# A Hedgehog linear-attention and MLP stack on one core: the query features scale only one of their two softmax halves, and every queue gets a new order

## The chip, the core and the metric

The kernel runs on one NeuronCore of a Trainium2 chip. Five engines work side by side, each through its own in-order queue: PE (TensorE, matrix products), DVE (VectorE), ACT (ScalarE), POOL (GpSimd) and SP (SyncE), which issues every DMA of this kernel. The metric is the device time of one launch in microseconds (us); lower is better. PEld in the rows is the loading of PE's weights, which overlaps its products.

## The reference

Four residual blocks on a (1, 2048, 512) input: attention, MLP, attention, MLP, with the same weights both times.

```python
def _A_ref(x, wqkv, w_phi, wo):
    H = 32; Dh = D // H          # D = 512, Dh = 16
    q, k, v = ...                # x @ wqkv, split by kind and head
    pq = jnp.einsum("bhsd,hdf->bhsf", q, w_phi)
    pk = jnp.einsum("bhsd,hdf->bhsf", k, w_phi)
    phi_q = jnp.concatenate([_softmax(pq, axis=-1), _softmax(-pq, axis=-1)], axis=-1)
    phi_k = jnp.concatenate([_softmax(pk, axis=-1), _softmax(-pk, axis=-1)], axis=-1)
    kv = jnp.einsum("bhsf,bhsd->bhfd", phi_k, v)
    z  = jnp.einsum("bhsf->bhf", phi_k)
    num = jnp.einsum("bhqf,bhfd->bhqd", phi_q, kv)
    den = jnp.einsum("bhqf,bhf->bhq", phi_q, z)[..., None] + 1e-6
    o = num / den
    return o.transpose(...).reshape(B, S, D) @ wo

def _B_ref(x, w1, w2):           # 512 -> 1792 -> 512
    return jnp.maximum(x @ w1, 0) @ w2

x = x + _A_ref(_layernorm(x), ...);  x = x + _B_ref(_layernorm(x), ...)
x = x + _A_ref(_layernorm(x), ...);  x = x + _B_ref(_layernorm(x), ...)
```

A head's output is a quotient: a factor on both softmaxes of a query's head scales num and den alike, and cancels but for the guard 1e-6.

## The kernel before

The 2048 rows are 16 chunks of 128 rows. A number is split into a high and a low float16 half, and a product is three matmuls of halves (PAIRS), so that PE works in float16. Names end in the layer l (0 or 1) and the chunk c or the tile t of two chunks.

- **First stage.** Weights come in and are split (fold, split); each chunk is normalised and turned, and gives keys (pk), values (pv) and queries (pq). The keys' features (feature_map with psum=True) and values are summed over all chunks into kv (gather). Of a value's product pv the high half is copied out by ACT (L791), PE then subtracts it with a matmul by "minus" (L795), and ACT copies the rest (L797).
- **Query features** (look, feature_map with psum=False; 32 of them). Queries wait in DRAM (q_dram) and come back as ql. DVE takes the maximum and minimum of each head's 16 numbers (L690, L691), shifts (L696); ACT takes the exponentials of the two halves (L708, two instructions); DVE sums each half and takes reciprocals (L714, L715); ACT multiplies the 64 reciprocals by PHI = 2^15 (L719); POOL multiplies all 1024 exponentials by them (L723); ACT rounds to the high half (L730), POOL takes the low half (L734), and SP turns the result by a DMA transpose (L578) into pT. PE multiplies it with kv (numerators, L1019, tile pn), and DVE adds the guard and divides (L1027 to L1030, tiles dn and o).
- **MLP.** For most tiles a seven-product scheme replaces eight block products (hidden_by_seven, L1433, bank ph; out_by_seven, L1608). Sums of weight blocks are built on POOL in the first tiles (sums_of_weight, L1289, and sums_of_second, L1326), stored in DRAM (s_dram, t_dram) and fetched per step by one 512 KB DMA (s, L1391) into one of three buffers; a load can go out once PE has read the sums three steps back. Sums of activations (n_t, n_u) are turned by DMA transposes into freed weight halves (wq_h, wq_l, wk_h, wk_l).
- **Order.** The order of each engine's queue is written out in the table ORDER, one digit a task: its place among the tasks still to come in the order in which the program made them. The class Plan merges the five queues, with its own estimate of each task (the numbers in add) and of each transfer (landing): a first time until a DMA lands, and a time by which it follows the one before. SP works strictly in order, so a DMA whose data isn't ready holds all behind it.
- **Buffers.** CAPS says how many tiles of a kind there are: two p16 (the features' halves, keys' and queries' alike), two e, three w2 (which hold s).

Of the kernel before, what the change touches and what calls it, by code (L numbers as in the profile page):

```python
# [18 lines left out]
P = 128  # L19
# [25 lines left out]
PHI = 2.0 ** 15  # L45
KV_S = 2.0 ** -26
# [35 lines left out]
        "22a002300024222817029200224007262110g2g2200201j02h3015022220b0228102a59010622002200211023100522220020102"
        "20021102000201023000342320022002000221022000010011010",
    ACT:
        "31201104220030005c5ba099fm088c306053cc10jj2902md2cj1003mZq320j141Zj0m2kZf0j1500k3k0j26gn2m5j1136312k3Mj4"
        "1222ll4010m10130h3021102301cc041gg310002801cc002060201bj2216312c1110k8jjd80g0f69da080d7c460307010aaa0301"
        "c0b0fa020c650400d40309gg18020b03600080740200100020850033494104501011403a3480262303201110141023500820a053"
        "032000020431012057115c53022201131020220251131303231010350243242021010142832204b4590302533333343350030004"
        "182b716191071018111222015261553544512362605599909808807cc0ccf00ef0ie00f0e2420a1d10b709250968073433a39383"
        "393570250a1912100510383067096106608533504321003044239a003305200550002041700122100605210643021004033020g0"  # L90
        "0e010524010504008d0770999051f05300322030014255016ecb101990u80607p067605v56060ep583m406I05G950D70Q677Zp6M"
        "6ZmL7777Zh805608043Zo44ZY032Zj04Zh4ZQ400011011040ZEf302ZQ52ZO4036311ZZjf33ZE110302224000ZZ31005042300030"
        "32200l605520052033135100f3ZG30141022010Ze22Zs0115044011102330006055246004030004140332501027011302B001044"
        "00014140220160j501360240306021g4021100222103020105042370501302070024400524401004003320030220030220030201"
        "03022103302040302200303321403020130220403305103000000",
# [48 lines left out]
class Plan:  # L144
# [32 lines left out]
    def landing(self, t):  # L177

        if t.turn:
            return 2.0 + t.kb / 220, t.kb / 230  # L180
# [1900 lines left out]
```

## Time and profile before

| | |
|---|---|
| median of 3 runs | 964.04 us (963.81 to 964.42) |
| the profiled execution's own time | 963.83 us |
| its span, first to last instruction | 962.1 us |
| between the two | 1.7 us |
| granted TensorE clock over the span | 1.000 of full speed (2.4 GHz) |
| PE, DVE, POOL, ACT busy | 98%, 72%, 67%, 60% of the span |
| DMA engines busy, moved | 74.3% in queue q1, 183.38 MB |

The profile has the engines' busy times, the waits (who waited for whom, the total, how often, the longest), the chain of waits that ended last (start, length, who), groups of instructions by line and shape, and timelines. An idle engine that nobody waits for costs nothing.

### The profile page before, as it was taken

What the parts mean: (1) busy time and instruction counts of PE and PEld (TensorE: products, weight loads), DVE (VectorE), ACT (ScalarE), POOL (GpSimd) and SP (SyncE); (2) the same over time, 40 slices, a digit from 0 to 9 for tenths busy, and PEclk for the clock granted to TensorE, in tenths of its full rate; (3) what the DMA queues carried; (4) which work ended last, traced back from release to release, by engine and by line L of the source; (5) the groups of instructions that cost most, each with busy time, mean ns of one, the idle gap of its engine ahead of it and who ended that gap; (6) DMA issues with size and microseconds to landing.
All of it is one profiled execution on the core that took longest, in us unless ns stands there. A gap on an engine that the chain in (4) does not pass through costs nothing.

```text
span 962.1 us, 23668 instructions
## 1 busy us (share of the span) xinstructions
PE 947.4 (98%) x9372; PEld 659.7 (69%) x9372; DVE 694.8 (72%) x1408; ACT 573.6 (60%) x1121; POOL 647.5 (67%) x634
## 2 busy tenths in 40 slices
PE   8999999999999999999999999999999999999997
PEld 5544555666665766566677775566666889888997
DVE  6899978856876877766566678987886575665455
ACT  7999978654554636454375555465555565555553
POOL 2699877778685857555376647267578888777644
PEclk9999999999999999999999999999999999999999
DMA  9387858499869697788649864599999786886541
GB/s 334 90 223 197 194 157 224 95 197 217 206 156 233 164 268 158 175 224 214 155 155 253 254 189 112 199 248 228 222 221 252 184 186 170 188 169 172 134 139 66
DMA packets 251807, 183.38 MB, mean 191 GB/s; under 512 B 180656, under 2 KB 188080, under 8 KB 251696
## 3 DMA queue, kind: packets, MB, share of 16 engines
q1 hardware_dynamic: 251696, 181.87, 74.3%
q8 instruction: 73, 1.20, 0.5%
q14 instruction: 38, 0.31, 0.1%
HBM read 108.30 MB, written 30.15 MB: 144 GB/s over the span
## 4 chain that ended last, share of the span: by engine, by line
PE 91%; DMA 2%; ACT 2%; POOL 2%; DVE 1%; issue 1%; SPq 0%; DVEq 0%; POOLq 0%; ACTq 0%
PE ph L1433 23%; PE py L1549 14%; PE py L1608 12%; PE pw L650 8%; PE pk L650 8%; PE pv L650 8%; PE pq L650 8%; PE ph L1513 3%; PE pn L1019 2%; PE kv L816 1%; DMA s<-s_dram 1%; DMA st_k<-in_A_wqkv_dram 1%; DMA wk_h<-n_u 1%; POOL sums L1289 0%; POOL p_q L734 0%
## 5 line engine op out<-in xcount | busy, mean ns | idle before, releaser
L1549 PE MATMUL py<-w,h 128*128 128x512 f16 x690 | 174.2, 379 | 0.0
L1433 PEld LDWEIGHTS <-s 128*128 128x128 f16 x2352 | 151.3, 98 | 28.3 <-DMA s<-s_dram 2.2
L1446 ACT ACTIVATE sn<-ph 128x128 f32<-128x128 f32 x294 | 80.6, 274 | 146.3 <-PE ph L1433 143.2
L650 PEld LDWEIGHTS <-xT 128*128 128x128 f16 x900 | 86.8, 98 | 99.1 <-DMA xT<-n_a 1.4
L1433 PEld LDWEIGHTS <-w 128*128 128x128 f16 x1764 | 111.0, 98 | 15.0 <-DMA wk_h<-n_u 1.4
L1433 PE MATMUL ph<-yT,s 128*128 128x128 f16 x1176 | 97.6, 219 | 1.1 <-DVE ph L1452 1.1
L1433 PE MATMUL ph<-yT,w 128*128 128x128 f16 x1176 | 97.6, 219 | 0.0
L1452 DVE TENSOR_TENSOR ph<-ph,sn 128x128 f32<-128x128 f32 x98 | 29.3, 299 | 92.3 <-PE ph L1433 48.5
L1549 PEld LDWEIGHTS <-h 128*128 128x128 f16 x690 | 61.4, 98 | 49.2
L734 POOL TENSOR_TENSOR p_q<-e_q,p_q 128x1024 f16<-128x1024 f32 x32 | 71.4, 2230 | 21.0 <-ACT p_q L730 21.0
L723 POOL TENSOR_TENSOR e_q<-e_q,fm_q 128x1024 f32<-128x1024 f32 x32 | 62.5, 1957 | 33.8 <-ACT fm_q L719 33.5
L734 POOL TENSOR_TENSOR p_k<-e_k,p_k 128x1024 f16<-128x1024 f32 x30 | 68.7, 2288 | 20.6 <-ACT p_k L730 20.5
L650 PE MATMUL pw<-wo_h,oT 128*128 128x512 f16 x256 | 81.4, 379 | 0.2 <-ACT qs L886 0.2
L650 PE MATMUL pk<-wk_h,xT 128*128 128x512 f16 x256 | 81.3, 379 | 0.0
L650 PE MATMUL pv<-wv_h,xT 128*128 128x512 f16 x256 | 81.2, 379 | 0.0
L723 POOL TENSOR_TENSOR e_k<-e_k,fm_k 128x1024 f32<-128x1024 f32 x30 | 59.5, 1983 | 28.7 <-ACT fm_k L719 27.7
L650 PEld LDWEIGHTS <-oT 128*128 128x128 f16 x384 | 37.0, 98 | 41.4 <-issue 1.0
L1457 DVE TENSOR_TENSOR ph<-ph,sn 128x256 f32<-128x256 f32 x98 | 41.9, 427 | 31.1 <-PE ph L1433 30.6
L1608 PEld LDWEIGHTS <-h 128*128 128x128 f16 x648 | 59.1, 98 | 6.4
L1229 POOL TENSOR_TENSOR w<-r 128x256 f32<-128x256 f32 x41 | 31.4, 766 | 40.0 <-ACT r L1225 40.0
L650 PE MATMUL pq<-wq_h,xq 128*128 128x512 f16 x168 | 56.6, 379 | 0.1
L1608 PE MATMUL py<-w,h 128*128 128x256 f16 x324 | 53.0, 273 | 0.0
(279 smaller groups left out, 2419.4 us busy)
## 6 DMA issues: line engine op xcount, KB each, us to landing
s<-s_dram SPq DMA_DIRECT2D x98, 512.0 KB, 4.4
q_dram<-qs SPq DMA_DIRECT2D x28, 256.0 KB, 3.8
ql<-q_dram SPq DMA_DIRECT2D x28, 256.0 KB, 3.7
u<-t_dram SPq DMA_DIRECT2D x13, 512.0 KB, 4.5
xt_dram<-xT SPq DMA_DIRECT2D x21, 256.0 KB, 4.2
xq<-xt_dram SPq DMA_DIRECT2D x21, 256.0 KB, 3.9
xe<-in_A_x_dram SPq DMA_DIRECT2D x16, 256.0 KB, 4.4
x<-in_A_x_dram SPq DMA_DIRECT2D x16, 256.0 KB, 4.2
```

The source lines that it names most:

```text
L650: nc.tensor.matmul(pm.ap, xT.ap[:, a, k, :], W.ap[b][:, k, :], start=(k == 0 and i == 0), stop=(k == KC - 1 and i == 2))
L723: (nc.vector if fast else nc.gpsimd).tensor_tensor(e3, e3, sm.unsqueeze(2).to_broadcast([P, 2 * n, DH]), op=ALU.mult)
L734: (nc.vector if fast else nc.gpsimd).tensor_sub(part16(1, cols), part16(1, cols, ef), part16(0, cols))
L1019: nc.tensor.matmul(at()[:, g, :], pT.ap[:, a, 4 * i + g, :], r[b].ap[:, 4 * i + g, :], start=(j == 0), stop=(j == 2))
L1229: nc.gpsimd.tensor_sub(rf.ap[:, :2, :], r.ap.rearrange("p (a b) -> p a b", a=4)[:, ::3, :], block(1).unsqueeze(1).to_broadcast([P, 2, P]))
L1433: nc.tensor.matmul(at(r), weight_of(i, b, kk, s, summed), rows_of(y, i, a, kk), start=(first and kk == 0 and n == 0), stop=(kk == 1 and n ...
L1446: nc.scalar.activation(saved(i), at(2), AF.Copy)
L1452: add(DVE, 0.27, lambda: nc.vector.tensor_tensor(at(3), at(1), saved(2), op=ALU.add), reads=[(ph, 1), (sn, 2)], writes=[(ph, 3)], boost=10 ...
L1457: add(DVE, 0.40, lambda: nc.vector.tensor_tensor(wide(ph), wide(ph), wide(sn), op=ALU.add), reads=[(sn, 0), (sn, 1)], writes=[(ph, 0), (ph ...
L1513: nc.tensor.matmul(at()[:, j, cs.start * P:cs.stop * P], W1.at(b, k, slice(f * P, (f + 1) * P)), yT.ap[:, cs, a, k, :], stop=(k == KC - 1 ...
L1549: nc.tensor.matmul(py.ap, h[a].ap.rearrange("p j t -> p (j t)")[:, cols], W2.at(b, fs[j], slice(0, D)), start=(begins and j == k == 0), st ...
L1608: nc.tensor.matmul(py.ap[:, 256 * r:256 * r + 256], left[a], right[b], start=(s == 0 and r == 0 and k == 0), stop=(last and k == 2), skip_ ...
```

## The change

For query features alone (not psum), the e tile is laid out by halves: all 32 first softmaxes (positive side), then all 32 second ones. With s1 and s2 the sums of the exponentials e1 and e2 of a head, it gives e1 * HALF and e2 * (s1 / s2 * HALF) in place of e1 * PHI / s1 and e2 * PHI / s2, with HALF = PHI / 16: both halves of a head times s1 / 16. The guard in the divide gets the same factor, from a small tile eps of 32 numbers a row. The constants of Plan.landing are new, and all five strings of ORDER. The keys' features keep their steps. Line numbers after L43 are higher in the new kernel.

```diff
+HALF = PHI / DH
 ORDER = {
     PE:
-        "000033222242210032000770204413339122603847310830209001180032710013140020331403160D516201xx12v04314031012"
+        "000052222522200001100770204413331802153847319030b20302901a02211013510600161013G0F051401411w203314q031036"
...
     def landing(self, t):
         if t.turn:
-            return 2.0 + t.kb / 220, t.kb / 230
+            return 1.6 + t.kb / 170, t.kb / 193
         if t.work > 1.5:
-            return 4.8, 2.4
-        return 1.6 + t.kb / 250, t.kb / 385
+            return 4.4, 2.5
+        return 1.8 + t.kb / 230, t.kb / 306
...
-            "statf": 2, "statb": 2, "fmf": 2, "fmb": 2, "dn": 2, "v": 2, "piece": 3,
+            "statf": 2, "statb": 2, "fmf": 2, "fmb": 2, "eps": 3, "dn": 2, "v": 2, "piece": 3,
...
         def part16(j, cols, x=None):
             if not psum:
-                return p16.ap[:, j, cols] if x is None else x
+                return (p16.ap[:, j, cols] if x is None else x).rearrange(
+                    "p (h s f) -> p h s f" if x is None else "p (s h f) -> p h s f", s=2, f=DH)
...
-                eh = e.ap[:, h:h + n]
+                eh = e.ap[:, h:h + n] if psum else e.ap.rearrange("p h s f -> p (h s f)").rearrange(
+                    "p (s h f) -> p h s f", s=2, f=DH)
...
+            def ratios(of=piece_of):
+                sm, e3 = of()[2], of()[5]
+                nc.vector.tensor_reduce(sm, e3, axis=AX.X, op=ALU.add)
+                nc.vector.reciprocal(sm[:, H:], sm[:, H:])
+                nc.vector.scalar_tensor_tensor(sm[:, H:], sm[:, :H], HALF, sm[:, H:], op0=ALU.mult, op1=ALU.mult)
+
+            def raised(of=piece_of):
+                e3 = of()[5]
+                nc.scalar.activation(e3[:, :H], e3[:, :H], AF.Copy, scale=HALF)
+
+            def guard(of=piece_of):
+                eps.ap = eps.make()
+                nc.scalar.activation(eps.ap, of()[2][:, :H], AF.Copy, scale=DEN_EPS)
...
             def product(of=piece_of):
                 _, _, sm, _, _, e3, _ = of()
+                if not psum:
+                    nc.gpsimd.tensor_tensor(e3[:, H:], e3[:, H:], sm[:, H:].unsqueeze(2).to_broadcast([P, H, DH]),
+                                            op=ALU.mult)
+                    return
...
+            if not psum:
+                add(DVE, 1.62, ratios, reads=[(e, h)], writes=[(fm, h)])
+                add(ACT, 0.55, raised, reads=[(fm, h)], writes=[(e, "+")])
+                p16.eps = eps = tiles(small, "eps", [P, H], F32, f"eps_{name}")
+                add(ACT, 0.162, guard, reads=[(fm, h)], makes=[eps])
+                add(POOL, 1.0, product, reads=[(fm, h)], writes=[(e, "-")])
+                add(ACT, 0.107 + 0.856 * u, high, reads=[e], makes=[p16])
+                add(POOL, 2.09 * u, low, reads=[e, p16], writes=[(p16, "l")])
+                continue
...
-            nc.vector.tensor_scalar(dn.ap[:, 0], at()[:, :, 64:], 1.0 / PHI, DEN_EPS * 16.0,
-                                    op0=ALU.mult, op1=ALU.add)
+            nc.vector.scalar_tensor_tensor(dn.ap[:, 0], at()[:, :, 64:], 1.0 / PHI,
+                                           eps.ap[:, 16 * i:16 * i + 16].rearrange("p (g h) -> p g h", g=4),
+                                           op0=ALU.mult, op1=ALU.add)
...
-        add(DVE, 0.827, divide, reads=[pn], makes=[dn, of] if i == 0 else [dn],
+        add(DVE, 0.827, divide, reads=[pn, eps], makes=[dn, of] if i == 0 else [dn],
```

PE's matmuls and SP's DMAs are the same in number and shape; their order isn't. Three places of it, of before and of the change apart, with rows left out that only repeat (a value, key or query product is 12 matmuls of 128x512).

**PE, end of the first stage.** pk, pv and pq are the products of keys, values and queries, kv0, kv1 and hb the sums over chunks; "minus" subtracts a value's high half. Before:

```order
L650 MATMUL pv_0_14_1598<-wv_h_115,xT_0_14_1509 128x512
L795 MATMUL pv_0_13_1511<-v1_108,minus_77 128x512
L816 MATMUL kv0_0_0_642<-v0_105,p16_k0_12_1580 128x66
L816 MATMUL kv1_0_0_650<-v0_105,p16_k0_12_1580 128x66
L816 MATMUL hb_0_0_658<-v0_105,p16_k0_12_1580 128x66
L795 MATMUL pv_0_14_1598<-v0_105,minus_77 128x512
L650 MATMUL pk_0_15_1647<-wk_h_113,xT_0_15_1612 128x512
```

The change:

```order
L651 MATMUL pv_0_14_1601<-wv_h_115,xT_0_14_1524 128x512
L828 MATMUL pv_0_13_1531<-v1_108,minus_77 128x512
L849 MATMUL kv0_0_0_634<-v0_105,p16_k0_12_1599 128x66
L849 MATMUL kv1_0_0_642<-v0_105,p16_k0_12_1599 128x66
L849 MATMUL hb_0_0_650<-v0_105,p16_k0_12_1599 128x66
L651 MATMUL pk_0_15_1647<-wk_h_113,xT_0_15_1615 128x512
L651 MATMUL pq_0_10_1672<-wq_h_111,xq_0_10_1262 128x512
L651 MATMUL pv_0_15_1692<-wv_h_115,xT_0_15_1615 128x512
L651 MATMUL pq_0_6_1727<-wq_h_111,xq_0_6_1484 128x512
L828 MATMUL pv_0_14_1601<-v0_105,minus_77 128x512
```

Between the products of chunk 14's values and the subtraction of their high half stood 17 matmuls; now three whole products and half of a fourth (12 + 12 + 12 + 6) stand there too.

**SP, layer 0, tile 5 of the MLP.** s_0_5_2 is the load of the third step's sums, yT and wq_h are DMA transposes. Before:

```order
L578 DMA_TRANSPOSE yT_0_6_5999<-n16_b0_12_5953 128x8x128
L1312 DMA seconds_6_6019<-in_B_w2_dram 128x2x512
L578 DMA_TRANSPOSE yT_0_6_5999<-n16_b0_13_5976 128x8x128
L1391 DMA s_0_5_2_6074<-s_dram_161 128x2x1024
L772 DMA xt_dram_103<-xT_1_6_5564 128x1024
L578 DMA_TRANSPOSE wq_h_111<-n16_t0_6_6053 128x8x128
L1050 DMA x_0_14_6111<-in_A_x_dram 128x512
L1391 DMA s_0_5_3_6154<-s_dram_161 128x2x1024
```

The change:

```order
L579 DMA_TRANSPOSE yT_0_6_6036<-n16_b0_13_6055 128x8x128
L1426 DMA s_0_5_2_6125<-s_dram_161 128x2x1024
L805 DMA xt_dram_103<-xT_1_7_5683 128x1024
L1085 DMA x_0_14_6146<-in_A_x_dram 128x512
L1426 DMA s_0_5_3_6206<-s_dram_161 128x2x1024
L1602 DMA x_dram_102<-x_0_8_3632 128x512
L1426 DMA s_0_5_4_6271<-s_dram_161 128x2x1024
L1602 DMA x_dram_102<-x_0_9_3952 128x512
L1426 DMA s_0_5_5_6302<-s_dram_161 128x2x1024
L579 DMA_TRANSPOSE wq_h_111<-n16_t0_6_6123 128x8x128
```

The transpose into wq_h, two rows behind the load of s_0_5_2, moved eight rows behind it.

**SP, layer 1, start of tile 2.** wk_h takes two transposes, n16_t and n16_u; the fourth product of ph_1_2_0 reads the second. Before:

```order
L578 DMA_TRANSPOSE wk_h_113<-n16_t1_2_10466 128x8x128
L1567 DMA out_0_dram<-x_1_1_7658 128x512
L1391 DMA s_1_2_0_10562<-s_dram_161 128x2x1024
L578 DMA_TRANSPOSE pT_1_10_10584<-p16_q1_10_10205 128x16x128
L1391 DMA s_1_2_1_10622<-s_dram_161 128x2x1024
L578 DMA_TRANSPOSE wk_h_113<-n16_u1_2_10547 128x4x128
```

The change:

```order
L579 DMA_TRANSPOSE pT_1_10_10583<-p16_q1_10_10313 128x16x128
L1426 DMA s_1_2_0_10621<-s_dram_161 128x2x1024
L579 DMA_TRANSPOSE wk_h_113<-n16_t1_2_10518 128x8x128
L579 DMA_TRANSPOSE yT_1_2_10315<-n16_b1_5_10511 128x8x128
L579 DMA_TRANSPOSE oT_1_8_10724<-n16_o1_8_10643 128x8x128
L1085 DMA x_1_8_10746<-x_dram_102 128x512
L1426 DMA s_1_2_1_10762<-s_dram_161 128x2x1024
L1030 DMA ql_1_14_10768<-q_dram_104 128x512
L579 DMA_TRANSPOSE wk_h_113<-n16_u1_2_10806 128x4x128
```

Between the two transposes into wk_h stood one transpose and three other DMAs; now two and three, and pT_1_10 is ahead of both.

## Rows read from the trace of the kernel before

**Rows 1.** The page: span, busy time and share of each engine.

```profile
span 962.1 us, 23668 instructions
PE 947.4 (98%) x9372; PEld 659.7 (69%) x9372; DVE 694.8 (72%) x1408; ACT 573.6 (60%) x1121; POOL 647.5 (67%) x634
```

**Rows 2.** Waits of PE: who for whom, total us, times, longest.

```profile
PE ph L1433 <- DMA s<-s_dram: 1.9, 2, 1.2
PE ph L1433 <- DMA wk_h<-n_u: 1.3, 1, 1.3
PE ph L1433 <- DVE ph L1452: 1.1, 3, 0.5
PE pv L795 <- ACT v L791: 0.7, 1, 0.7
PE pw L650 <- ACT qs L886: 0.2, 1, 0.2
```

**Rows 3.** Chain of waits, first stage: start us, length us, what.

```profile
20.69 2.59 PE pv L650 x12
...
127.18 0.61 ACT v L791
```

**Rows 4.** Timelines of POOL, then ACT, 177 to 190 us: start, us, instruction.

```profile
177.52 2.70 POOL L723 TENSOR_TENSOR e_q<-e_q,fm_q 128x1024 f32<-128x1024 f32 x1 [0.86 <-ACT fm_q L719]
184.71 3.48 POOL L1289 TENSOR_TENSOR sums<-sums 128x256 f32<-128x256 f32 x2
188.22 1.15 ACT L1279 ACTIVATE sums_h<-sums,s_w 128x1024 f16<-128x1024 f32 x1 [3.18 <-POOL sums L1289]
189.28 0.58 ACT L886 ACTIVATE qs<-pq 128x512 f32<-128x512 f32 x1
```

**Rows 5.** Chain of waits, 374 to 386 us, layer 0 tile 4.

```profile
374.59 0.07 PE kvn L816 x2
...
381.41 4.38 DMA s<-s_dram
```

**Rows 6.** Chain of waits, then SP's timeline, from 431 us, tile 5.

```profile
431.67 6.37 DMA s<-s_dram
...
432.64 1.48 SPq L578 DMA_TRANSPOSE wq_h<-n_t  x1
```

**Rows 7.** SP's timeline, then the chain of waits, 719 to 732 us.

```profile
718.98 1.24 SPq L578 DMA_TRANSPOSE wk_h<-n_t  x1
...
721.96 3.74 SPq L578 DMA_TRANSPOSE pT<-p_q  x1
725.79 0.53 SPq L1391 DMA_DIRECT2D s<-s_dram  x1
...
726.42 5.60 DMA wk_h<-n_u
```

**Rows 8.** Groups by line and shape: xcount | busy us, mean ns | idle before.

```profile
L734 POOL TENSOR_TENSOR p_q<-e_q,p_q 128x1024 f16<-128x1024 f32 x32 | 71.4, 2230 | 21.0 <-ACT p_q L730 21.0
L723 POOL TENSOR_TENSOR e_q<-e_q,fm_q 128x1024 f32<-128x1024 f32 x32 | 62.5, 1957 | 33.8 <-ACT fm_q L719 33.5
L715 DVE RECIPROCAL fm_q<-fm_q 128x64 f32<-128x64 f32 x32 | 17.7, 553 | 1.1
L564 ACT ACTIVATE n_o<-o 128x512 f16<-128x512 f32 x28 | 17.5, 626 | 12.4 <-DMA oT<-n_o 7.0 <-DVE o L1030 3.7 <-issue 1.3
L1027 DVE TENSOR_SCALAR dn<-pn 128x16 f32<-128x16 f32 x64 | 10.7, 167 | 8.9 <-PE pn L1019 8.6
L719 ACT ACTIVATE fm_q<-fm_q 128x64 f32<-128x64 f32 x32 | 8.0, 251 | 8.8 <-DVE fm_q L715 8.6
```

**Rows 9.** Busy time by stretch, 48 to 72 us: PE, PEld, DVE, ACT, POOL.

```profile
48.00:72.00 24.00, 24.00 (x155) 11.87 (x154) 21.61 (x41) 21.94 (x35) 23.01 (x17) 1.00 0.83 221
```

**Rows 10.** Timeline of ACT, then DVE, around 8.6 us.

```profile
8.64 1.06 ACT L387 ACTIVATE wk_l<-st_k 128x1024 bf16<-128x1024 f32 x1 [1.67 <-DMA st_k<-in_A_wqkv_dram]
...
8.91 0.69 DVE L1708 TENSOR_TENSOR bd<-phi,mask 128x512 f32<-128x512 f32 x1 [3.25 <-DMA phi<-in_A_w_phi_dram]
```

More of the change, by code (lines that the diff above doesn't have):

```diff
@@ new lines @@
+        "00730671360043022110000002110000004000002000000000000000050060dd00h000j00k000000000000000000000001141112"
+        "22222222220333333330222333403333302222220000000001112222011022800b00000000050000002000043000000000000000"
+        "111110000305000000000000000000050060dd00h0000000f00000d0f00000000000000000000222220111111333333333334445"
+        "55044444444444133022233344444444666055505555566677788888aaa090800666666070660555504444444133022100000000"
+        "00000000000000000001111110110000111110011111403333330222250444444033333022666666666605999080702242021000"
@@ L103 @@
[L103 to L108 removed]
+        "33030222100f3332221336211001di0302920g435811a21000c10a00Z0Z0d0hc00eS044e4dMg66Je0g5004c40302h20fi111f00l"
@@ new lines @@
+        "1020b1a4080200i0220e11c1w00040r00103m023q3p252m40KK09IP9O2007K05Z9Z906Z70303452b333026Z3ZB12Z10610ZuWZt9"
+        "13i7i002Zu0Zt130i21Zng000g0100ZK1ZJb0100ZE16007l11041h101110l11Zt023Zqg0005423Zi210a29200b25017022i40022"
+        "002b2002h310402322813092006220026625010f2f200220j023g7010332010a2920020107262520020002200231005222210201"
+        "0201022102000220022110223220022002210220301000010011010",
+    ACT:
+        "31011104221022105cc5a0a9n20l8c70a7610cl20j2930d2cjj114Zs0u301jj14nnZh03qZf8302m5l1k10n26mm2k511361l24j14"
+        "101H2kk411011042g0f251002205bb0g1hh31000201ee60023002401bj314251d212108llld80i0hh69b0880e74c460037010bb0"
+        "a3f220j20318f61675806002001830676c1039990bb810023557000b17066700500730103212504b454173740343030112241300"
+        "01327b06034001000204120120915716c44043022200404031260560054044200400234322302000051234261140393302650234"
+        "32220224102300181b100012010000400323409627751654451383077c71a66898991e810b1b01d910bccff0e24200e900b0a620"
+        "a748456444aa448039357753b3a330073c651180070250605013211302220410442a309083302720500020400424222046104004"
+        "303110061551k4101g118213512115500088c0bc0b69689010d304200000510012130f20418a0a700t79089440l6l604505q3478"
+        "al0lK73i0G9G08T073A77Zq06045I55ZiH5ZhF6696Zb4404ZnZZ103021Zi4ZiZS4Zgr41ZO4553ZZ10702ZF5003p0524422041ZG3"
+        "ZG12ZZf1133300030220050233210Zh3033o200ZJ60551163044071020g40ZH322102221Zh0302Zt010504403500032110055521"
+        "052440010451032252138001H002220050g42201030301l17005i140052440703600f00210302224030000504427052002207035"
+        "040602442000400330140302040022003022140022003302003022210303220002220002225103020413000000",
@@ new lines @@
+    SP:
+        "2000101026007a0d009A21089006t8670461H0202312GF3152623be512110n605j6220gtz4511451008af00f0g2l210ss122c5k2"
+        "21321yi1H2141jb11c911a3e4c5a41424263a12822882p2a66666d9b7o5946265h5529955s18c3fh78587e67a3a480i5650e1807"
+        "3272a6767ach8423a984265h5238844827b8e9f32d0a1a5330caTa340931160999a5868709014405033352488jA2736464131s23"
+        "0o615363672iv32E511i00bt237v400g2051t009x1w1b0a0abA0420d3C0g6a00463E918bI1Sg8307587054dO4m421a86R114k964"
+        "14Q312211004g504304603132200074030d2524604412a00040330244624433005511555514413551133000010",
@@ L739, in feature_map @@
             add(ACT, 0.171 + 0.884 * u if psum else 1.23, exps, reads=[inv, *([] if psum else [neg])], writes=[(e, h)])
+            if not psum:
+                add(DVE, 1.62, ratios, reads=[(e, h)], writes=[(fm, h)])
[6 more added lines that the diff above has]
+                continue
             add(DVE, 0.2 + 1.52 * u, sums, reads=[(e, h)], writes=[(fm, h)])
```

71 lines of the change are left out of this document (24 added, 47 removed).

## The prediction

> **What bounds the kernel now.** I read the page's totals first, then PE's waits, then the chain that ended last, and at each wait the timeline of the engine it names. PE is busy 947.4 of 962.1 us [rows 1]; 14.7 us are left, opening and end included. Whether the 947.4 has room inside is told by the chain: twelve matmuls of 512 columns take 2.59 us [rows 3], 216 ns each, which is one column a cycle at 2.4 GHz, and the granted clock is 1.000. They stand back to back, and the change leaves their number and shape alone. So only PE's waits can be won. Inside the stages they are five [rows 2]: 1.9 (DMA s) + 1.3 (DMA wk_h) + 1.1 (DVE ph) + 0.7 (ACT v) + 0.2 (ACT qs) = 5.2 us. The rest of the 14.7 is the opening and the last tile's end. The profiled execution took 963.83 us, 1.7 over its span; the median lies 0.2 above it. With all five waits gone it would be 958.6.
>
> **The new arithmetic, for each of 32 query maps** [rows 8].
> - POOL's product falls from 1024 to 512 elements a row. It took 1957 ns; half is 0.98 us, and a fixed part of each instruction would make it more, at most some 1.2 (estimate: half, plus 251 ns, the whole of a small ACT instruction, as the fixed part). I take 0.98. POOL loses 32 x 0.98 = 31 us of 647.5.
> - ACT loses the scaling of reciprocals (251 ns) and gains "raised", 512 elements: 626 ns by the rounding of n_o, the nearest shape; and the guard, 32 elements, at most the 251 of 64. Net +0.5 to +0.63 us a map; I take 0.6, so +19 us of 573.6.
> - DVE's reciprocal goes from 64 to 32 elements: 553 ns becomes 277 to 553. The new small ratio of 32 elements is near the 167 ns of a 16-element divide step. Net −0.1 to +0.2; I take 0.
> - The divide's first step gets a tensor in place of a constant, still 16 elements: 167 ns as before, bounds 0 to 0.1 more. DVE idles 28% of the span.
> - High and low halves keep their counts; the query e is now read in 32 pieces of 16 elements that lie apart. The old product, which also stepped by sixteens through its factors, took 1957 ns and the low half 2230, so I take no change; bound, +10% on both.
>
> On the path of one map from exponentials to p_q: −0.25 (scaling) −0.98 (product) ± 0.2 (DVE); "raised" runs on ACT beside the product. So p_q is ready about 1.2 us earlier. None of this is PE's work: it counts only where PE waits on this path. What hides ACT's extra 0.6 is ACT's idle time: in 48 to 72 us it is busy 21.94 of 24.00 with PE at 24.00 [rows 9], so 2.06 us are free there and up to four maps of the changed kernel add 2.4.
>
> **The order, wait by wait.** The time PE has ahead of a need is counted from the two orders, matmuls between release and need at 216 ns for 512 columns, smaller ones in proportion.
> - **ACT v, 0.7.** PE stood 0.61 us at 127.18 [rows 3] for the high half of chunk 14's values, with 17 matmuls between, 12 of them of only 66 columns. Now 42 more of 512 columns stand there, 9.07 us. Gone: −0.7.
> - **ACT qs, 0.2.** At 189.28 qs came right behind sums_h, for which ACT idled 3.18 us on POOL's sums; those stood behind a product of 2.70 and a sums step of 3.48 [rows 4]. In the new order that product is halved, and two sums steps go ahead of work that preceded them. At least 1.35 us come from the halving alone. Gone: −0.2.
> - **DMA s, 0.7 of 1.9, tile 4.** The chain runs from the last kvn (374.59) over ACT, POOL's low half and SP's transpose to the s load of 4.38 us [rows 5]. From that kvn to the need PE had 48.5 matmuls, 10.48 us; now 59.8, 12.92. Gone: −0.7, even if the map gained nothing.
> - **DMA s, 1.2 of 1.9, tile 5.** This load took 6.37 us, and a transpose into wq_h was issued 1 us behind it [rows 6]; the load in rows 5 took 4.38. The transpose moves eight rows back, and the cover grows from 10.34 to 10.73. If the transpose was what slowed it, 2.0 come back and all 1.2 goes; if not, 0.4 goes. I take the middle, −0.8.
> - **DMA wk_h, 1.3.** The turned n_u landed 5.60 us after issue. Ahead of it SP spent 1.24 on the first transpose and 3.74 on that of p_q, plus two plain loads [rows 7]. The new order puts two transposes and three plain DMAs there: 2 x 1.24 at best, 2 x 3.74 at worst, and 3 x 0.53 for the plain ones (the row of s), so 4.1 to 9.1, against 6.2 from the end of the first transpose (720.22) to 726.42. PE's cover grows from 8.98 to 11.58. Worst: 9.1 − 6.2 − 2.6 = +0.3; best, all gone. I take −0.9.
> - **DVE ph, 1.1.** Two of its three are at the end, where the rows are the same. No change.
>
> Rows 6 and 7 say that a DMA transpose costs its neighbours. The Trainium skill, "Advanced Engine Details and Errata", § X-Bar Transpose (TRN2), says the opposite: such transposes are as fast as regular DMAs. By that rule moving them gains nothing by itself, the tile-5 load wins 0.4 in place of 0.8, and the sum is 0.4 higher. No row here shows two transfers of one size, one of each kind, so it isn't settled.
>
> Together −0.7 − 0.2 − 0.7 − 0.8 − 0.9 = −3.3.
>
> **What the new order adds.** Every queue is new, so new holds can arise. SP issues 140 transposes in both orders, but with another transpose right behind in 35 places instead of 25. A held load cost 0.7 to 1.3 here [rows 2]. I found no one place where a cover falls under what its load took, but rows of before can't show all; I take one hold of the smaller price, +0.7 (bounds 0 to three of 1.3). At the opening the new order has ACT square phi (landed by 8.91) ahead of the split of st_k (8.64) [rows 10], and PE waits there for both: 0 to 1.06, the length of that split; I take +0.2.
>
> Sum: 963.83 − 3.3 + 0.7 + 0.2 = 961.4; with the 0.2 to the median, **961.6 us**.
>
> **Rivals.**
> 1. *Holds only move; same.* PE's waits for loads depend on which transpose happens to be in SP's queue; the three load waits (3.2) come back elsewhere under the new order, and only ACT v and ACT qs go: 964.04 − 0.9 = 963.1, up to 964 with the opening. For it: 35 pairs against 25, and POOL, which gains most, is busy only 67% and named in no wait of PE [rows 1, 2]. Against it: covers grew at all three loads. The Trainium skill, "Perfetto Trace Analysis", § Identifying Performance Opportunities, has the same as a general rule, that one improves the most contended engine; by it the arithmetic wins nothing, as I also have it, and only the order counts.
> 2. *SP's queue holds three loads more; slower.* With transposes in pairs, SP spends 3.74 on the second instead of 1.24 [rows 7], a load behind it goes out 2.5 later, and PE stands for up to 1.3. It decides from three such new holds, if the old load waits also stay: 963.1 + 3 x 1.3 = 967.0. Against: the covers at the three that I could follow.
> 3. *ACT becomes the bound from 24 to 96 us; same.* Four maps in 24 us with "raised" and the guard at their upper prices add 4 x 0.63 = 2.5 to 2.06 free [rows 9]: 0.45 over, in three such stretches 1.3: 961.6 + 1.3 = 962.9. For it: the first stage is ACT's and POOL's densest. Against: one such stretch of three is all I have a row for, and queues between can carry it.
> 4. *The change doesn't do what it says; same.* If pieces of 16 make ACT's high half and POOL's low half slower by what the product saves (0.98), p_q comes no sooner: qs and part of tile 4's gain go, some +0.4, and ACT's cost stays: 962.4 to 963.
>
> **How the numbers follow.** About 0.2% (1.9 us) is what a measurement of this kernel can tell from no change, so the bounds are 962.1 and 966.0. Forecast, 960 to 962.1 or below: 0.54. Rivals 1, 3 and 4, all inside the bounds: 0.24 + 0.06 + 0.05 = 0.35. Rival 2: 0.11. Faster 0.54, same 0.35, slower 0.11. Low end: all five waits but DVE's gone (4.1), no new hold, and 1 us more of what lies in the opening: 964.04 − 5.1 = 958.9, and 0.4 below that for what I missed, 958.5. High end: 966.0 is where slower begins; half of the way on to rival 2's 967.0 gives 966.5. About 0.08 are left out above it and 0.1 below 958.5.
>
> **What would show it.** In the trace after: the product of 128x512 in 32 rows of about 0.98 us, "raised" about 0.6, the guard at most 0.25, POOL near 617 busy and ACT near 593, PE unchanged at 947 with fewer idle us. In PE's waits no ACT v, no ACT qs, DMA s under 1.0 and wk_h at most 0.5. If DMA waits stay near 3.2 with other tiles named, rival 1 holds; if SP's second transposes of a pair are named ahead of new waits, rival 2; if ACT is named as what PE waits for between 24 and 96 us, rival 3; if high and low take over 10% longer, rival 4. A new wait at the opening over 1 us, or any single new hold over 2 us, would make the number wrong.

## The result, and the profile after

| | before | after |
|---|---|---|
| median, 8 runs each | 964.12 us (962.68 to 965.35) | 967.73 us (965.69 to 971.10) |
| ratio to before, 95% interval | | 1.0036 (1.0024 to 1.0048) |
| the profiled execution's own time | 963.83 us | 965.69 us, the shortest of its 8 |
| its span | 962.1 us | 963.7 us |

The change makes the kernel 0.36% slower, some 3.5 us. The forecast was 961.6 with a range up to 966.5: wrong in its sign and in its range. "Slower" had been given 0.11.

The page of the profile after, which answers [rows 1]:

```profile
span 963.7 us, 23721 instructions
PE 948.5 (98%) x9372; PEld 658.7 (68%) x9372; DVE 703.8 (73%) x1440; ACT 589.3 (61%) x1153; POOL 618.3 (64%) x634
```

The engines did what was expected of them: POOL lost 29.2 us, ACT gained 15.7. The groups of the query features after (line, engine, shape, xcount | busy us, mean ns), to be read beside [rows 8]:

```profile
L758 POOL TENSOR_TENSOR p_q<-e_q,p_q 128x1024 f16<-128x1024 f32 x32 | 70.7, 2209 | 28.8 <-ACT p_q L754 25.3 <-DMA oT<-n_o 2.1 <-DVE ph L1487 1.2
L744 POOL TENSOR_TENSOR e_q<-e_q,fm_q 128x512 f32<-128x512 f32 x32 | 34.0, 1062 | 42.5 <-DVE dn L1061 24.3 <-ACT eps_q L735 8.3 <-DVE fm_q L727 6.9
L731 ACT ACTIVATE e_q<-e_q 128x512 f32<-128x512 f32 x32 | 20.0, 624 | 1.1 <-DVE fm_q L725 1.0
L727 DVE SCALAR_TENSOR_TENSOR fm_q<-fm_q 128x32 f32<-128x32 f32 x32 | 11.6, 363 | 1.1
L726 DVE RECIPROCAL fm_q<-fm_q 128x32 f32<-128x32 f32 x32 | 11.3, 353 | 1.1
```

PE's waits after (who for whom: total us, times, longest), beside [rows 2]; first of the profiled execution of 965.69 us, then of a second one of the same kernel, 967.33 us, which is nearer to the median:

```profile
PE pw L651 <- DMA oT<-n_o: 1.3, 3, 0.7
PE ph L1468 <- DVE ph L1487: 1.2, 4, 0.5
PE pq L651 <- DMA xq<-xt_dram: 0.9, 1, 0.9
PE py L1643 <- POOL w L1264: 0.7, 2, 0.3
PE ph L1548 <- DVE yT L603: 0.6, 1, 0.6
PE pk L651 <- DMA xT<-n_a: 0.5, 2, 0.3
```

```profile
PE pw L651 <- DMA oT<-n_o: 2.0, 4, 0.7
PE pq L651 <- DMA xq<-xt_dram: 1.8, 1, 1.8
PE ph L1468 <- DVE ph L1487: 1.2, 4, 0.5
PE py L1643 <- POOL w L1264: 0.7, 2, 0.3
PE ph L1548 <- DVE yT L603: 0.6, 1, 0.6
PE ph L1468 <- DMA s<-s_dram: 0.5, 2, 0.3
```

The waits on ACT v and on wk_h are gone, and DMA s fell from 1.9 to 0 and 0.5. In their place stand oT (the turned attention output), xq (reloaded inputs for queries), w (sums of the second layer) and yT, none of which the view of before names. Without the opening the view adds up to 5.4 us before, 5.9 in the first and 7.7 in the second profile. So the old waits went, and more than as many new ones came.

The waits aren't the whole loss. PE's idle time, 14.7 us in before, is 15.2 and 16.9 us; its busy time rose as well, by 1.1 us (947.4 to 948.5, in both profiles), with as many matmuls and a granted clock of 1.00 in each 1 us stretch up to 960 us; and between the span and the time lie 2.0 and 1.9 us in place of 1.7. Idle, busy and end give 0.5 + 1.1 + 0.3 = 1.9 and 2.2 + 1.1 + 0.2 = 3.5, which is by how much the two executions are longer than the 963.83 of before. Why the busy time rose was not tried. An estimate: a matmul of 512 columns takes 379 ns by itself and 216 back to back, so each hold shows some 0.16 us more of busy time behind it, and 23 holds are listed in place of 15, which makes 1.3. Of the runs below e2 (42 holds, 951.9 us busy) fits this, e3 (16 holds, 950.2) doesn't.

### The profile page after: what moved, and what is told of

Its sections match the earlier page's. It is cut to its first block, busy times and chain, and to the rows that moved or that the text cites. A ratio compares the mean times of both kernels' runs of the same rounds, so it can differ in the third digit from the quotient of the medians.

```text
span 963.7 us, 23721 instructions
## 1 busy us (share of the span) xinstructions
PE 948.5 (98%) x9372; PEld 658.7 (68%) x9372; DVE 703.8 (73%) x1440; ACT 589.3 (61%) x1153; POOL 618.3 (64%) x634
## 4 chain that ended last, share of the span: by engine, by line
PE 78%; DMA 6%; POOL 5%; DVE 5%; ACT 3%; issue 2%; SPq 0%; DVEq 0%; POOLq 0%; ACTq 0%
PE ph L1468 21%; PE py L1584 13%; PE py L1643 11%; PE pw L651 8%; PE pk L651 6%; PE pv L651 5%; PE pq L651 5%; PE ph L1548 4%; DMA oT<-n_o 2%; PE pn L1053 2%; POOL p_k L758 1%; POOL e_k L747 1%; DMA w<-in_B_w_dram 1%; POOL n_a L568 1%; DVE fm_q L725 1%
## 5 line engine op out<-in xcount | busy, mean ns | idle before, releaser
L1487 DVE TENSOR_TENSOR ph<-ph,sn 128x128 f32<-128x128 f32 x98 | 29.2, 298 | 88.9 <-PE ph L1468 52.7
L758 POOL TENSOR_TENSOR p_q<-e_q,p_q 128x1024 f16<-128x1024 f32 x32 | 70.7, 2209 | 28.8 <-ACT p_q L754 25.3
L744 POOL TENSOR_TENSOR e_q<-e_q,fm_q 128x512 f32<-128x512 f32 x32 | 34.0, 1062 | 42.5 <-DVE dn L1061 24.3
```

The source lines that it names most:

```text
L744: nc.gpsimd.tensor_tensor(e3[:, H:], e3[:, H:], sm[:, H:].unsqueeze(2).to_broadcast([P, H, DH]), op=ALU.mult)
L758: (nc.vector if fast else nc.gpsimd).tensor_sub(part16(1, cols), part16(1, cols, ef), part16(0, cols))
L1487: add(DVE, 0.27, lambda: nc.vector.tensor_tensor(at(3), at(1), saved(2), op=ALU.add), reads=[(ph, 1), (sn, 2)], writes=[(ph, 3)], boost=10 ...
```

## The experiments

Each run was timed in rounds against the kernel before, on one chip per group. The medians of before in the four groups were 963.2, 963.4, 963.75 and 964.0, so ratios are what to compare. "Old order" is that of before, translated task by task; "new order" that of the change. The theories at the start: ORDER, the new holds belong to the new queues; ARITHMETIC, the longer ACT work or the changed reads hold PE.

| run | order | arithmetic | median us | ratio (95%) |
|---|---|---|---|---|
| e0 | new | new | 967.33 | 1.0041 (1.0024 to 1.0059) |
| e1 | old | new, guards stall ACT | 970.02 | 1.0064 (1.0046 to 1.0083) |
| e2 | new | old | 989.31 | 1.0265 (1.0241 to 1.0288) |
| e3 | old | new, six guard tiles | 967.83 | 1.0039 (1.0025 to 1.0054) |
| e4 | old | new, without raised | 966.67 | 1.0034 (1.0022 to 1.0046) |
| e5 | new | new, without raised | 965.61 | 1.0026 (1.0015 to 1.0036) |
| e6 | new | new, product twice in all 32 maps | 976.89 | 1.0140 (1.0122 to 1.0158) |
| e7 | old | e4, product twice in 3 maps | 963.53 | 0.9995 (0.9983 to 1.0008) |
| e9 | old, one PE row moved | as e7 | 963.04 | 0.9990 (0.9980 to 0.9999) |
| e8 | new, two SP rows moved | new | 967.46 | 1.0039 (1.0024 to 1.0053) |
| e10 | as e9, one SP row moved | as e7 | 962.97 | 0.9991 (0.9978 to 1.0005) |
| e11 | new, last stage as before | new | 970.38 | 1.0063 (1.0045 to 1.0080) |

### The two halves of the change apart (e1, e2), and the change again (e0)

Edit of e1: the changed kernel, ORDER translated from before, landing as before, and

```diff
-            ... "eps": 3, "dn": 2, ...
+            ... "eps": 4, "dn": 1, ...
```

> The new arithmetic of the query features in the order of before: raised and the guard stand where the scaling of reciprocals stood, with three guards moved 6 to 9 tasks later on ACT, four eps tiles and one dn tile. Theory ORDER (the new holds come from the five new queues): PE's waits of before stay or shrink, since each map's features are ready about 1 us sooner: 962.5 to 964.2 us, median clock 1.000 in all runs. Theory ARITHMETIC (the longer ACT work or the spread-out reads of e hold PE): 966 to 969 us, with ACT or POOL named in PE's waits.

Edit of e2: the kernel before with the new ORDER and landing; ups stands where raised stood, in two maps 10 and 24 ACT tasks ahead of that.

> The old arithmetic in the new order, two of the 32 scalings moved 10 and 24 tasks earlier on ACT. Theory ORDER: the holds of the changed kernel stay, and as each map is ready about 1 us later some grow: 966 to 970 us, and some executions with a granted clock under 1.000. Theory ARITHMETIC: 962 to 964.5 us.

> The changed kernel once more. Its runs went from 965.7 to 971.1, the longer ones with a granted clock of 0.997 to 0.999. Theory HOLDS (all of the loss is PE's waits): the profile shows more waits in the longer runs and the clock is a by-product worth under 0.5 us. Theory CLOCK (part of the loss is the clock): the profile of a longer run shows a stretch of PE at a granted clock under 1.0, right after a wait of PE, worth 1 to 5 us. Median expected 966 to 968.5 under both.

Measured: 970.02, 989.31 and 967.33. Both halves alone are slower than before. The new order with the old arithmetic is far slower than the two together; the new arithmetic in the old order isn't clearly so (its interval overlaps e0's, and e3 below gives 1.0039). Neither ORDER nor ARITHMETIC holds by itself. It looks as if an order is fitted to the durations of one arithmetic; e6 and e7 try that. PE's longest wait in either half is on sn, ACT's copy of a product of the MLP, which PE did not wait for beyond 0.2 us in before. Of e1, then of e2:

```profile
PE ph L1468 <- ACT sn L1481: 4.9, 6, 1.8
```

```profile
PE ph L1433 <- ACT sn L1446: 10.2, 12, 1.9
```

A part of e1's loss was made by the run itself: with four guard tiles ACT stood for a divide before it could write a guard. From ACT's waits in e1:

```profile
ACT eps_q L735 <- DVE dn L1061: 10.3, 4, 3.7
```

Two of the four, 3.7 and 2.8 us, stand in ACT's queue ahead of the sn copies that PE waited for at 730 and 769 us.

In e0 four of the seven executions had a mean granted clock of 1.000 and took 967.3 to 968.6 us; five executions of before with that clock, in the same rounds, took 961.8 to 964.8. So the loss is there without a lower clock. What a lower clock adds in the longer executions stays open: the profile that was kept is of one at 1.000.

### What the arithmetic does in the old order (e3, e4), and in the new (e5, e6)

e3 takes the guards' stalls away; e4 takes raised away as well, by putting its factor into the exponential:

```diff
-eps = tiles(small, "eps", [P, H], F32, f"eps_{name}")
+eps = tiles(small, "eps", [P, H], BF16, f"eps_{name}")     (e3: six; e4, e5: five)
```

```diff
-nc.scalar.activation(eh[:, :, side, :], eh[:, :, side, :], AF.Exp, scale=by.ap)
+nc.scalar.activation(eh[:, :, side, :], eh[:, :, side, :], AF.Exp, scale=by.ap, bias=lnhalf)   (side 0)
-nc.vector.scalar_tensor_tensor(sm[:, H:], sm[:, :H], HALF, sm[:, H:], op0=ALU.mult, op1=ALU.mult)
+nc.vector.tensor_tensor(sm[:, H:], sm[:, :H], sm[:, H:], op=ALU.mult)
-add(ACT, 0.55, raised, reads=[(fm, h)], writes=[(e, "+")])
```

> As the first run of the arithmetic in the order of before, but with six guard tiles (in bfloat16, so that they fit), so that ACT never waits for a divide before it writes a guard; there it stood 10.3 us in four such waits. Theory RAISED (ACT's 0.62 us of raised a map stands in ACT's in-order queue ahead of sn, the copy of an MLP product that PE waits for): 966 to 968.5 us, sn still named with 2 to 4 us. Theory GUARD (the loss of that run was its own stalls on guard tiles): 962 to 964 us, sn under 1 us.

> The order of before, the new ratio, but no raised at all: the first half's exponential gets the factor as a bias, exp(x + ln HALF), so ACT has nothing added. Only POOL's product is halved and the scaling becomes the guard. Theory RAISED: with ACT's addition gone the order of before fits again, 961 to 963.5 us, no sn over 0.5 us. Theory GUARD: the same as the run beside it within 1 us.

> The new order with the same arithmetic without raised: 32 x 0.62 us of ACT taken away. Theory HOLDS (the new waits come from where loads and transposes stand in SP's queue): the waits on xq, oT and w stay, 965.5 to 967.5 us. Theory RAISED alone (ACT's addition is what the new order could not place): 962 to 964.5 us.

e6 is the changed kernel with

```diff
 nc.gpsimd.tensor_tensor(e3[:, H:], e3[:, H:], sm[:, H:].unsqueeze(2).to_broadcast([P, H, DH]), op=ALU.mult)
+nc.gpsimd.tensor_tensor(e3[:, H:], e3[:, H:], ones[:, :H].unsqueeze(2).to_broadcast([P, H, DH]), op=ALU.mult)
```

> The changed kernel with POOL's product done twice (the second time by ones): 32 x 1.06 us of POOL given back, so POOL is as before. If the halving is worth nothing here (POOL off PE's path): 966.5 to 968.5 us, as the changed kernel. If the new order leans on it: 970 to 985 us, with waits on what POOL makes (oT, pT, w) grown.

Measured: 967.83, 966.67, 965.61, 976.89. e4 is the surprise. It has the old order, ACT's work as before (574.0 us against 573.6) and 27.5 us less on POOL (620.0), and is still 0.34% slower; expected were 961 to 963.5. Both theories of e3 and e4 fall, though e3's time is the one that RAISED gave (its wait on sn, 1.7, is less): neither the guards' stalls nor raised is the main loss. e5 came out as HOLDS said: with ACT's work near that of before (575.4 us) the waits on oT (2.5), xq (1.0) and w (0.7) stay in the new order. Raised itself is worth 0.5 us between e3 and e4 by the ratios and 1.4 between e0 and e5; the intervals overlap in both pairs, so that it costs anything is likely and not shown. e6 says the other thing: given POOL's time back, the new order loses 9.5 us. It leans on the saving, but not by the waits that were expected to grow: in e6's profile oT fell to 0.7, w kept its 0.7, and of the three only pT grew (1.5), beside sn (2.1), s (2.0), xq (1.9) and DVE's o (1.6). That e2 loses another 12 us is not explained.

### Where e4 lost: DVE's shift and POOL exclude each other (e7)

PE's new waits in e4 stand at 627, 658 and 677 us, on ACT. Followed back, ACT waited there for DVE, and DVE was in the shift of a query map (e_q from ql). From e4's waits of PE, the first line the one at 627, the second those at 658 and 677:

```profile
PE pq L654 <- ACT qs L924: 1.6, 1, 1.6
PE ph L1473 <- ACT sn L1486: 1.8, 2, 1.0
```

POOL's and DVE's timelines are put together here in pairs (start us, us, instruction), first a pair of the kernel before, then three of e4:

```profile
267.02 2.13 POOL L734 TENSOR_TENSOR p_q<-e_q,p_q 128x1024 f16<-128x1024 f32 x1
267.37 2.86 DVE L696 TENSOR_TENSOR e_q<-ql,fm_q 128x1024 f32<-128x1024 f32 x1
```

```profile
621.84 2.13 POOL L764 TENSOR_TENSOR p_q<-e_q,p_q 128x1024 f16<-128x1024 f32 x1 [1.17 <-ACT p_q L760]
622.50 2.55 DVE L705 TENSOR_TENSOR e_q<-ql,fm_q 128x1024 f32<-128x1024 f32 x1
650.21 2.13 POOL L764 TENSOR_TENSOR p_q<-e_q,p_q 128x1024 f16<-128x1024 f32 x1 [1.17 <-ACT p_q L760]
650.47 2.96 DVE L705 TENSOR_TENSOR e_q<-ql,fm_q 128x1024 f32<-128x1024 f32 x1
674.02 2.13 POOL L764 TENSOR_TENSOR p_q<-e_q,p_q 128x1024 f16<-128x1024 f32 x1 [1.17 <-ACT p_q L760]
674.20 3.03 DVE L705 TENSOR_TENSOR e_q<-ql,fm_q 128x1024 f32<-128x1024 f32 x1
```

An undisturbed shift takes 1.21 to 1.23 us. In each pair it ends 1.08 or 1.09 us after POOL's instruction (in the first, 267.37 + 2.86 less 267.02 + 2.13), whatever its own start: it stands until POOL is done, and the profile shows the standing as busy time of DVE. In the fourteen traces 104 shifts took over 1.3 us, and each ended 1.08 or 1.09 us after the POOL instruction that ran when it began. Now look at before at the same place as the pair at 621:

```profile
619.87 1.93 POOL L723 TENSOR_TENSOR e_q<-e_q,fm_q 128x1024 f32<-128x1024 f32 x1 [16.58 <-ACT fm_q L719]
622.97 2.38 POOL L734 TENSOR_TENSOR p_q<-e_q,p_q 128x1024 f16<-128x1024 f32 x1 [1.17 <-ACT p_q L730]
```

```profile
622.13 1.22 DVE L696 TENSOR_TENSOR e_q<-ql,fm_q 128x1024 f32<-128x1024 f32 x1
```

The product of 1.93 ended 1.17 us of ACT before the low half could begin, at 622.97, and the shift went first at 622.13. With the halved product the low half begins at 621.84, 0.66 ahead of the shift, and holds it. That is a theory that can be tried by adding work:

```diff
+TWICE = ('q1_2', 'q1_5', 'q1_7')
 nc.gpsimd.tensor_tensor(e3[:, H:], e3[:, H:], sm[:, H:].unsqueeze(2).to_broadcast([P, H, DH]), op=ALU.mult)
+if name in TWICE:
+    nc.gpsimd.tensor_tensor(e3[:, H:], e3[:, H:], ones[:, :H].unsqueeze(2).to_broadcast([P, H, DH]), op=ALU.mult)
```

> The run with the factor as a bias in the order of before (966.67), with one thing changed: for three of the 32 maps, layer 1 chunks 2, 5 and 7, POOL does its product twice (the second time by ones), which adds 3 x 1.06 us of work and takes none away. In that run POOL's low half of these maps began 0.2 to 0.7 us before DVE was ready to shift the next map, and DVE's shift took 2.5 to 3.0 us in place of 1.2. Theory EXCLUSION (the shift and a POOL instruction don't run at once, and a shorter product lets POOL slip in first): the shifts are 1.2 us again, and the waits at 627, 658 and 677 us shrink: 963 to 965 us, 2 to 3.5 less for more work. Theory WORK (time follows the work of the engines): 966.7 to 968 us.

Measured: 963.53, 0.9995 in place of 1.0034, with 3.2 us more work on POOL. The first of the three places in e7, POOL's rows and then DVE's:

```profile
620.74 1.06 POOL L751 TENSOR_TENSOR e_q<-e_q,fm_q 128x512 f32<-128x512 f32 x1 [16.20 <-ACT oT L603]
621.87 1.06 POOL L754 TENSOR_TENSOR e_q<-e_q,ones 128x512 f32<-128x512 f32 x1
624.10 2.32 POOL L768 TENSOR_TENSOR p_q<-e_q,p_q 128x1024 f16<-128x1024 f32 x1 [1.17 <-ACT p_q L764]
```

```profile
623.21 1.22 DVE L706 TENSOR_TENSOR e_q<-ql,fm_q 128x1024 f32<-128x1024 f32 x1
```

EXCLUSION is shown: three extra products bring the three shifts back to 1.21 to 1.23 us, the three waits on ACT (3.4 us) are gone from e7's profile, and 3 to 4 us with them. e3, with raised, has the same three shifts (2.84 to 3.04 us) and waits of 1.6, 0.7 and 1.0 at them.

It works the other way round too. In the changed kernel's first profile DVE is first, and POOL's low half, 2.13 us when undisturbed, ends 1.99 us after DVE's instruction:

```profile
87.67 2.08 DVE L445 SCALAR_TENSOR_TENSOR w<-w,s_w,w 128x1792 f16<-128x1792 f32 x1
87.92 3.82 POOL L758 TENSOR_TENSOR p_k<-e_k,p_k 128x1024 f16<-128x1024 f32 x1 [0.74 <-ACT p_k L754]
```

### Repairs of single holds (e9, e10; e8, e11)

e9 is e7 with PE's subtraction behind the next product, e10 is e9 with a transpose moved on SP:

```diff
-L795 MATMUL pv_0_14<-v,minus
 L650 MATMUL pk_0_15<-wk_h,xT x12
+L795 MATMUL pv_0_14<-v,minus
```

```diff
+L578 DMA_TRANSPOSE wk_h<-n16_u1_2
 L578 DMA_TRANSPOSE pT_1_10<-p16_q1_10
 L1391 DMA s_1_2_1<-s_dram
-L578 DMA_TRANSPOSE wk_h<-n16_u1_2
```

> The same, and PE's subtraction of chunk 14's high half moved behind the keys' product of chunk 15 (one row of PE's order). Theory: PE's 0.85 us hold at 127 us goes and nothing else moves: 0.6 to 0.9 us under the run beside it, 962 to 964.4. Rival (the wait behind it moves up, since what PE does next waits for the same copies): no change.

> The second run of the collisions undone (963.0), with one row of SP's order moved: at layer 1, tile 2, the transpose of n_u into wk_h goes ahead of the transpose of p_q of chunk 10 (3.8 us on SP) and the load of s behind that. POOL had n_u ready at 721.0, SP took it at 725.9. Theory TRANSPOSE QUEUE (the hold of 1.3 to 2.0 us at 730 is SP's time on the transpose ahead): the hold goes, 1 to 2 us less where it stood, 961 to 962.5 us. Rival (the transpose of p_q and the load of s then come late instead): a new wait on pT or s_1_2_1 of over 1 us, no change in the time.

Measured: 963.04 (0.9990) and 962.97 (0.9991). The wait on ACT v is gone from e9's profile; the median gained 0.5 us where 0.6 to 0.9 were expected, and the intervals of e7 and e9 overlap, so the gain isn't shown. In e10 the wait on wk_h is gone, which stood in e9's profile with 1.8 us:

```profile
PE ph L1477 <- DMA wk_h<-n_u: 1.8, 1, 1.8
```

The time stayed the same, against TRANSPOSE QUEUE; the rival's new wait on pT or s_1_2_1 didn't come either, but one of 1.0 us on xT did, at 106 us. e7's profile, with the same rows on SP as e9, doesn't have this wait either: it comes in some executions only, and what one profile shows of it isn't what the median pays.

e8 and e11 repair the changed kernel. e8:

```diff
+L910 DMA xq_0_10<-xt_dram
+L910 DMA xq_0_5<-xt_dram
 L579 DMA_TRANSPOSE xT_0_11<-n16_a0_11
-L910 DMA xq_0_10<-xt_dram
-L910 DMA xq_0_5<-xt_dram
```

> The changed kernel with two rows of SP's order moved: the loads of xq_0_10 and xq_0_5 ahead of the transpose of xT_0_11, which waits for POOL until 93.4 us. Theory SP ROW (the 1.1 to 2.0 us hold on xq at 99 us is SP's in-order queue, and where it is longest it lowers the clock as well): hold gone, 1 to 2 us less, 965 to 966.5 us, and runs over 969 us gone. Rival (the loads then wait for the store of chunk 10 and hold the transposes behind them, so that PE waits for xT): 967 to 968.5 us.

e11 puts the tasks made from number 4150 on into the old order among the places that they hold in the new one.

> The changed kernel, with the order of before among the tasks of the last stage (those made from number 4150 on; from about 780 us), 199 places of the five queues. Theory PIECES (the new order's small holds belong to each stretch by itself): the holds at 880, 903 and 945 us (0.3 + 0.5 + 0.5, on s and on w from POOL) go, at most the two of before at 821 and 825 come (0.3 + 0.2): 0.5 to 1.3 us less than the changed kernel's 967.4. Rival (a hold in the last stage comes from how far the stages ahead have got): no change or more.

Measured: 967.46 (1.0039) and 970.38 (1.0063). In e8 the wait on xq is gone from PE's waits, and the time is what it was: in that stretch wo_l (0.3) took over, and oT kept its 1.3. Two of its eleven executions were still over 969 us (969.2 and 972.0). In e11 the waits at 880, 903 and 945 us went as expected, and one on oT of 2.5 us came at 864:

```profile
PE pw L651 <- DMA oT<-n_o: 4.3, 4, 2.5
```

The chain there, in e11 (start us, length us, what):

```profile
857.59 1.50 POOL n_b L568
859.09 1.43 POOL n_o L568
860.52 0.51 POOL ts L1125
861.03 6.11 DMA oT<-n_o
```

So the last stage's order couldn't be exchanged by itself. The time is as that run's rival said; that the new hold comes from how far the stages ahead had got was not followed up.

## Why the prediction was wrong

**The five waits.** Right. Those on ACT v, on wk_h and on s at 385 and 437 us are gone in both profiles of the change; 0.2 on qs stands at another place (144 us), and in the second s stands with 0.3 at most, at other places. The sum of −3.3 was sound, if small: all 4.1 went. Tile 5's load, 6.37 us in before, landed 4.1 us after its issue in both profiles, with the transpose no longer behind it: the better of the two cases whose middle was taken. One place doesn't show that the transpose did it.

**The arithmetic's prices.** Mostly right. The product took 1.062 us, not 0.98, within the bound of 1.2. Raised 0.624 and the guard 0.22 were as said. DVE's reciprocal and ratio take 353 + 363 = 716 ns in place of 553, +0.16 within −0.1 to +0.2. High and low stayed (1054 and 2209 ns): rival 4 fell. In 48 to 72 us PE is busy 24.00 of 24.00 and ACT 22.85, so rival 3 fell too.

**"p_q is ready about 1.2 us earlier ... it counts only where PE waits on this path."** This step failed for the arithmetic by itself; it isn't what made the changed kernel slow, which the next paragraph has. It took an earlier POOL to be harmless at worst. The shift of another map on DVE and POOL's instruction exclude each other, so an earlier low half can go in front of a shift and put DVE 1.3 to 1.8 us back, and PE, behind ACT, 0.8 to 1.6. Three such places made the old order 3 to 4 us slower with less work on POOL and no more on ACT (e4 against e7). The trace of before had it to read: a shift of 2.86 us at 267 beside 1.22 (seven of its 32 took over 1.3), and Plan keeps tasks marked "lock", the shift among them, apart from POOL's. The Trainium skill, "SBUF — State Buffer", § SBUF: two separate sides, says that VectorE and GpSimd share a pair of ports that one of them holds for its whole instruction while the other stands; the pairs above agree, with 1.08 us from POOL's end to the shift's end.

**"One hold of the smaller price, +0.7."** This is the step that failed in the changed kernel: the term of the sum for what the new order adds was put at 0.7 and measured 4.7 to 6.5. Waits inside the stages that before didn't have, on oT, xq, w, yT, xT and h, add up to 4.3 us in the profile of 965.69 and to 5.8 in that of 967.33; with qs, pT and s at their new places it is 4.7 and 6.5. No single one is above 1.8. The bound that I gave, three of 1.3, was 3.9. Beside it, "PE unchanged at 947" put at nothing the 1.1 us by which PE's busy time rose. The shifts don't explain it: the new order's 32 take 1.29 us in the mean, those of before 1.35 and of e4 1.46. I looked for a place whose cover fell under what its load took and found none; the holds came instead at a dozen places where a cover was short by 0.2 to 0.9 (first profile). The largest, xq, stands behind a transpose on SP whose input POOL makes. That transpose and the first product of xq, in before and then in the first profile of the change:

```profile
93.53 1.24 SPq L578 DMA_TRANSPOSE xT<-n_a  x1
102.97 0.38 PE L650 MATMUL pq<-wq_h,xq 128*128 128x512 f16 x1
```

```profile
93.40 1.24 SPq L579 DMA_TRANSPOSE xT<-n_a  x1
100.23 0.39 PE L651 MATMUL pq<-wq_h,xq 128*128 128x512 f16 x1 [0.92 <-DMA xq<-xt_dram]
```

POOL and SP were no later than in before, and the two loads of xq landed sooner (99.5 and 100.2 us; 100.3 and 101.6 in before). PE came to its first product of xq at 99.3 in place of 103.0: what fell short is the cover, which PE's new order made 3.7 us smaller.

**The opening.** Right in size: waits of 4.5 us in all before, 4.5 and 4.7 after.

**The rivals.** Rival 1, "holds only move", is what happened, but it was held to an even exchange, 963.1 to 964. The exchange was worse than even by 0.5 to 2.3 us in the waits view, and by 3.5 in the median. Rival 2 (SP's pairs of transposes) wasn't seen as I priced it. Its 3.74 us [rows 7] is a transpose of 128x16x128, twice the size of the one that took 1.24, and in before such a one takes 3.05 in the median with no transpose ahead of it: I read as a matter of place what is one of size. In the first profile of the change twelve smaller transposes went right behind another, ten of them in 1.25 to 1.56 us, two in 2.3 and 2.4. And where a load stood behind a transpose, xq at 99 us, SP was waiting for the transpose's data from POOL and not for its length, and moving the load ahead (e8), or a transpose out from behind another (e10), gained nothing in the median.

**What is settled, and what isn't.** Shown: the arithmetic without its own order is slower, by the exclusion for the most part (e4, e7); the changed kernel's loss lies in PE's new holds and, by 1.1 us, in its busy time, by the two profiles; the new order needs the shorter product (e6); and with the collisions undone in the old order the arithmetic without raised is even with before, or 0.1% better (e9). Not shown: that taking the holds out gives the time back (e8 took out the largest and gained nothing in the median), and why the new order's covers are short on oT and w. A suspect is in the diff: by landing a 256 KB transpose comes in 1.6 + 256/170 = 3.1 us, and at 291 us oT took 4.71 (5.25 at 469). But the old constants give 3.2, and no order was made with longer ones, so this wasn't tried.

e9 is the one version of the twelve that beats both kernels, before by 0.0010 (0.0001 to 0.0020), which is less than the 0.2% that one measurement can tell.

## What to carry to other kernels

An order written out for in-order queues is fitted to the durations that it was made with: make one instruction shorter, and others collide that used to pass each other, so time the new arithmetic and the new order each without the other before believing in either. When POOL's work is cut or moved, look for VectorE instructions that take twice their usual time beside it: that is standing time shown as busy time, and in which of the two went first lay more here than the cut was worth. The waits that go can be read off a trace; for the waits that a reordering brings, take the total of those that it removes as the first estimate, not one of them: here 4.3 us went, and 4.7 and 6.5 came.

## What the runs showed of the hardware

That a shift of DVE stands until POOL's instruction is done, and is then 1.08 us from its end, is above. The other thing is PE's clock after a hold. In e7's profile PE stood 1.6 us for the weights of the queries (st_q) until 16.2 us, and the granted clock then fell to 0.50, the 1.2 GHz level, for 3 us. Busy time by stretch (us: PE, PEld, DVE, ACT, POOL; then the granted clock, DMA share, GB/s):

```profile
16.00:17.00 1.00, 0.78 (x6) 0.78 (x7) 0.87 (x2) 1.00 (x2) 0.02 (x1) 0.89 0.96 394
17.00:18.00 1.00, 1.00 (x6) 0.65 (x5) 1.00 (x3) 1.00 (x3) 0.00 (x0) 0.50 1.04 430
18.00:19.00 1.00, 1.00 (x4) 0.36 (x3) 1.00 (x3) 1.00 (x2) 0.00 (x0) 0.50 0.97 392
20.00:21.00 1.00, 1.00 (x6) 0.45 (x5) 0.00 (x0) 0.00 (x0) 0.00 (x0) 0.90 0.99 396
```

In e6 the same followed a wait of 1.9 us on xq that ended at 101.7 us: 0.50 from 103 to 106 us.

```profile
103.00:104.00 1.00, 1.00 (x7) 0.42 (x5) 1.00 (x3) 0.60 (x1) 0.53 (x1) 0.50 0.90 350
104.00:105.00 1.00, 1.00 (x4) 0.30 (x2) 1.00 (x3) 0.08 (x1) 0.00 (x0) 0.50 0.41 117
```

But after waits of 1.8 us in the second profile of the changed kernel, of 2.2 at the opening in e5's, and of 2.4 and 2.5 in e11's, no stretch of 1 us in the 50 us behind them was under 1.00. By these rows a hold of about 2 us can cost its length and some 1.5 us more (an estimate: 3 us at half the clock), and not in every execution. The longest run of the changed kernel, 971.1 us, had a mean granted clock of 0.997, the shortest 1.000; how much of its spread this makes up was not measured.
